# First two token tiles normalised one by one with ScalarE's square root, zero matmuls between their transposes, K and Q of the first eight heads alone, and a new issue order

## The chip, the cores and the metric

The kernel runs on one core of a Trainium2 chip. The metric is the device time of one execution in microseconds, less is better. Three runs of the kernel before gave 477.39, 476.0 and 477.12; their median is 477.12. The profile shows one execution, its times counted from its first instruction.

## The reference, cut to what matters

Two layers run over 2048 tokens of width 512. Each layer is an attention block (A) and a gated feed-forward block (B), with a layer normalisation ahead of either and a residual added behind it. The same weights serve both layers.

```python
def _layernorm(x):
    m = jnp.mean(x, axis=-1, keepdims=True); v = jnp.var(x, axis=-1, keepdims=True)
    return (x - m) / jnp.sqrt(v + 1e-05)

def _A_ref(x, wq, wk, wv, wo, beta):          # 32 heads of 16, N = 4 segments of L = 512 tokens
    q, k, v = ...                             # (B, H, N, L, 16)
    g = sigmoid(beta)
    for s in range(N):
        p = softmax(q_s k_s^T * scale + causal mask)
        o = g * (phi(q_s) M / (phi(q_s) z)) + (1 - g) * (p v_s)
        M, z = M + phi(k_s)^T v_s, z + sum phi(k_s)
    return concat(o) @ wo

def _B_ref(x, w1, w3, w2):                    # F = 1376
    return (silu(x @ w1) * (x @ w3)) @ w2

x = x + A(layernorm(x)); x = x + B(layernorm(x))      # layer 1
x = x + A(layernorm(x)); x = x + B(layernorm(x))      # layer 2
```

## The kernel before, in words

**The queues.** The kernel is written as a list of operations, each with the data that it reads and writes. Two texts then fix everything: `ORDER` gives the order in which all 3629 operations are issued, and `OTHER` names those that go to the second of their two allowed engines. (Emptying a PSUM bank, `ev`, may be done by ScalarE or by VectorE.) Each engine works through its own part of the list strictly in that order, and waits on semaphores ("lanes") for what the other engines owe it. There are 24 lanes: one for each of four engines, and eight for each queue that issues transfers (four in ScalarE's case). At the end SP waits once for every lane, sorted by lane number; a lane has its number from its first use. The last store to the output uses the lane numbered 11, so twelve lanes are waited for behind it.

**The stages.** Tokens go in segments of 512 (four tiles of 128), four segments in each of two layers. For each segment: layer normalisation; the transposed rows; Q, K and V (`project`); attention; output projection; normalisation; feed-forward. Work of neighbouring segments is interleaved by `ORDER`.

**Attention.** The heads are four groups G of eight. A unit is a batch of scores for 512 columns: TensorE (L897) writes them into PSUM, ScalarE takes the exponential (L906), GpSimd masks the diagonal blocks (L919), TensorE multiplies with V (L948). In the first segment a unit is cut in two halves of 1024 columns a row, and the segment's tokens are taken in two parts (tiles 0 and 1, then 2 and 3). There are 180 exponentials in all. The first unit reads K and Q of G = 0 and G = 1, with tiles 0 and 1.

**The head of the kernel**, which the change is about, runs so:

- Tiles 0 to 3 of x and the weights `wk` and `wq` are fetched. Later loads (tiles 4 to 7, `wv`, `w1`, `w3`, `wo`) are issued by SP once the third tile's statistics are done.
- Meanwhile TensorE multiplies zeros: seven operations `spin` of two 512-column matmuls (L524).
- `layer_norm(fine=True)` takes the tiles in pairs: VectorE's statistics (L635, L637) of both tiles, plus 1e-5 (L641), GpSimd's power -0.5 (L644), VectorE's two normalisations (L653), TensorE's four 128-column transposes for each tile (L665), and two copies out of PSUM, one on ScalarE (L493) and one on VectorE (L494).
- `project(first=True)` computes K and Q for tiles 0 and 1 with 256 columns a matmul (L226), two groups G to a bank: four jobs of eight matmuls. Banks are emptied by ScalarE (L493) or VectorE (L494); a masked copy of K for the odd heads (`km`, L738) is made by VectorE.
- ScalarE's own list begins: copy of tile 0's transposes, tanh for the gate (L615), K of G = 0, 1, Q of G = 0, 1, then exponentials.

Of the kernel before, what the change touches and what calls it, by code (L numbers as in the profile page):

```python
# [4 lines left out]
ALU = mybir.AluOpType  # L5
# [50 lines left out]
class Sched:  # L56
# [144 lines left out]
    def emit(self, nc, block):  # L201
# [49 lines left out]
def o_pe(ns):  # L251
# [7 lines left out]
    24 8 1 23 26 25 28 27 29 4 0 16 9 2 5 3 18 10 6-7 11 17 19 12 22 20-21 32 13-14 30 15 33 31 34 42 35 55 54 36  # L259
    56-58 39 37 43 40 38 41 44 84 45-47 51 65 94 66-68 75-76 69-70 77 71-72 78-82 85-91 61 73 83 74 163-164 161-162  # L260
    95 52 96-98 165 108-109 169-170 48 92 49 93 652 648 171 53 646 110 99-100 175 111 103 101 50 102 59-60 172 177
    650 176 166 123 178 124 167 112 168 173 180 179 104-105 181 113-114 182 653 649 651 647 654 115 183 125-126 106
    197 116-120 184 142 213 143 107 121 198 214 344 62 174 187 655 122 337 144 189 127-130 199 190 665 659 185
    200-201 131 145-146 132-137 211 660-661 138-140 235 151-153 212 236 186 345 233 203 348 147 202 204 662 346 350
    191 656 205 234 239-240 216 188 237 241-242 154 148 243 156 244 155 217 247 157 218-219 158 249 149 159 657 248
    250 150 160 251-252 717-720 663 666 238 658 253 215 347 245 255-256 664 667-671 349 721 352 141 257 63 192 353
    246 351 254 258 701 225 259 702 261 260 672 206 226 193-194 263 195 262 271-272 722 1080 264 207 1086 209 273-274
    208 1082 703-704 275 723 210 279 354-355 276 1084 1087 1081 1085 1083 280 673 277 724-725 285 674 278 675 281 356
    286 1088 220 705 1089 284 357 221 223 222 726 227 265 287 289 297 679 290 64 228 1093 229 1094 266 288 298 1091
    299 690 1090 196 691-692 300-302 693-694 684 303-304 1095 231 230 306 680-681 282 682 307-308 676 309 685-686 305  # L270
    310 224 683 677 687-688 311 695 678 696-698 706-707 1092 325 312 689 323 315 712 862 732 326 324 283 708-709 313
    291 699 314 267 232 733 736 734 710 316 292 1096 713-714 327-328 864 269 715-716 711 1097 749 329 1098-1099
    1106-1109 293-295 750 358-359 317 330 735 752-753 865 331 268 270 360 296 755 754 1100 361 1126 866 363 868 318
    737 362 364-367 1110 1127-1129 756 727-730 1111-1112 368 370 332 1130 371 369 861 757 319 1161 1113-1114 731 333
    863 342 372 738 760 1145-1148 1150 739 758 334 759 1115 1151-1152 867 761 1149 373 335 1153 1131 763 1132
    1121-1122 1140 1154 1160 740 321 336 320 322 375 764 751 1141-1142 1123 1143 1124 872 767 1133-1134 1144 1125 873
    374 1162 768 869-870 1135 741-742 376 1155-1156 1292 1157-1159 743-744 770 766 765 762 1101-1105 1136-1137 1139
    871 774-775 771 1290 1289 1293 377-378 784 379-380 382-385 381 785 1138 341 339 786 772-773 787 776 1291 777 700
# [123 lines left out]
def build(nc, A_x, A_wq, A_wk, A_wv, A_wo, A_beta, B_w1, B_w3, B_w2, out):  # L402
# [771 lines left out]
```

## Time and profile before

| what | value |
|---|---|
| median of three runs | 477.12 us (476.0 to 477.39) |
| span of the profiled execution | 476.0 us |
| time of that execution | 476.0 us, the span itself; one of the three runs shows the same figure |
| TensorE busy | 469.3 us, 99% |
| ScalarE busy | 390.6 us, 82% |
| VectorE busy | 385.3 us, 81% |
| GpSimd busy | 235.2 us, 49% |
| first exponential starts | 11.68 us |

Busy shares are means over stages with different limits. TensorE's ends are modelled (a matmul counts until its result has left the array), so that short gaps of it don't show as idle time. What bounds a stage is read from the chain of work in that stage and from who waits there.

### The profile page before, as it was taken

Reading aid. Unit: us, or ns where it says so; the run is one execution under the profiler, and the core shown is the slowest. Engines: PE = TensorE matmul, PEld = TensorE weight load, DVE = VectorE, ACT = ScalarE, POOL = GpSimd, SP = SyncE. Lnnn points to the kernel's source line nnn. Section 1 sums busy time; section 2 is a strip of 40 time slices with the busy share of each in tenths; the row PEclk is TensorE's granted clock in tenths of the full one; section 3 lists DMA queues with packets and bytes.
Section 4 is the critical chain, followed back from the end, with each engine's and each line's share of the span. In section 5 each row is a group of like instructions: output and inputs, shape, how many; then the busy total and the mean of one; then the engine's idle time right before and its main releaser. Section 6 shows DMA issues by size and latency. Waiting matters only on the chain.

```text
span 476.0 us, 14319 instructions
## 1 busy us (share of the span) xinstructions
PE 469.3 (99%) x6161; PEld 225.1 (47%) x6161; DVE 385.3 (81%) x818; ACT 390.6 (82%) x350; POOL 235.2 (49%) x382
## 2 busy tenths in 40 slices
PE   8999999999999999999999999999999999999997
PEld 4543456754443444444444344444444444444554
DVE  6899999897987977888987888787986677588582
ACT  2999999988999998999979999888989987930220
POOL 4756467746466556365464644644454655320000
DMA  8753349634134343251344416333132213332501
GB/s 263 265 101 74 66 91 195 113 67 56 23 68 90 68 90 62 48 84 36 67 83 85 68 24 107 63 68 64 31 64 44 45 34 67 69 39 48 119 14 56
DMA packets 106526, 37.14 MB, mean 78 GB/s; under 512 B 99200, under 2 KB 104448, under 8 KB 106464
## 3 DMA queue, kind: packets, MB, share of 16 engines
q1 hardware_dynamic: 104016, 31.41, 33.5%
q0 software_dynamic: 1488, 4.03, 3.9%
q8 instruction: 48, 0.79, 0.7%
q10 hardware_dynamic: 960, 0.79, 0.5%
q14 instruction: 14, 0.11, 0.1%
HBM read 8.43 MB, written 2.10 MB: 22 GB/s over the span
## 4 chain that ended last, share of the span: by engine, by line
PE 80%; ACT 11%; issue 3%; DVE 2%; DMA 2%; POOL 0%; POOLq 0%; DVEq 0%; SPq 0%
PE psall L226 48%; PE psall L231 15%; ACT e L906 9%; PE psall L897 9%; PE psall L948 6%; PE psall L524 1%; ACT px L755 1%; DMA W<-xn 1%; DMA xg<-xs 1%; PE psall L782 0%; DVE gp L1065 0%; DVE h L1069 0%; DVE W L759 0%; DVE xn L653 0%; ACT th L1063 0%
## 5 line engine op out<-in xcount | busy, mean ns | idle before, releaser
L906 ACT ACTIVATE e<-psall 128x2048 bf16<-128x2048 f32 (+1 forms) x180 | 300.5, 1697 | 26.1 <-PE psall L897 24.4
L919 POOL TENSOR_SCALAR_AFFINE_SELECT e<-e 128x512 bf16<-128x512 bf16 x256 | 157.5, 639 | 145.0 <-ACT e L906 97.5
L226 PE MATMUL psall<-W,w 128*128 128x512 bf16 (+1 forms) x499 | 106.9, 351 | 0.0
L226 PEld LDWEIGHTS psall<-W,w 128*128 128x128 bf16 x499 | 45.1, 98 | 44.4 <-issue 5.9
L1065 DVE SCALAR_TENSOR_TENSOR gp<-th,psall 128x512 bf16<-128x512 bf16 x80 | 54.0, 682 | 12.9 <-ACT th L1063 12.1
L1069 DVE SCALAR_TENSOR_TENSOR h<-gp,psall 128x512 bf16<-128x512 bf16 x80 | 54.0, 681 | 10.5 <-PE psall L226 6.3
L1063 ACT ACTIVATE th<-psall 128x512 bf16<-128x512 f32 x80 | 46.9, 600 | 16.1 <-PE psall L231 15.0
L226 PE MATMUL psall<-w,h 128*128 128x512 bf16 (+1 forms) x212 | 53.9, 380 | 0.0
L231 PE MATMUL psall<-W,w 128*32 128x512 bf16 (+1 forms) x884 | 48.8, 367 | 0.0
L635 DVE BATCH_NORM_STATS2 ln<-x_tok 128x6 f32<-128x512 bf16 x64 | 43.0, 686 | 1.7 <-DMA x_tok<-in_A_x_dram 1.0
L494 DVE CAST W<-psall 128x512 bf16<-128x512 f32 x51 | 34.6, 683 | 10.4 <-PE psall L226 9.9
L897 PE MATMUL psall<-W 16*128 16x256 bf16 (+3 forms) x544 | 41.3, 294 | 0.3
L948 PE MATMUL psall<-e,va 128*32 128x256 bf16 (+3 forms) x1088 | 41.2, 292 | 0.3 <-DVE rm L811 0.2
L897 PE MATMUL psall<-W,km 32*128 32x256 bf16 (+3 forms) x544 | 40.8, 291 | 0.0
L981 POOL TENSOR_TENSOR og<-xg,rd 128x256 bf16<-128x256 bf16 (+1 forms) x50 | 27.2, 559 | 24.4 <-DVE rd L975 16.6
L1088 DVE TENSOR_TENSOR x_tok<-psall,x_tok 128x512 bf16<-128x512 f32 (+1 forms) x33 | 21.7, 669 | 20.6 <-PE psall L231 11.1
L948 PEld LDWEIGHTS psall<-e,va 128*32 128x32 bf16 x1088 | 26.0, 96 | 17.5 <-issue 3.3
L231 PE MATMUL psall<-w,h 128*32 128x512 bf16 (+3 forms) x604 | 34.3, 364 | 0.0
L231 PEld LDWEIGHTS psall<-W,w 128*32 128x32 bf16 x884 | 23.4, 97 | 18.9 <-DVE h L1069 1.0
L494 DVE CAST xs<-psall 128x512 bf16<-128x512 f32 x40 | 26.7, 680 | 5.7 <-PE psall L948 5.6
L226 PE MATMUL psall<-wv,W 128*128 128x512 bf16 x110 | 31.3, 381 | 0.0
L897 PEld LDWEIGHTS psall<-W 16*128 16x128 bf16 x544 | 13.1, 91 | 37.8 <-ACT e L906 29.6
(85 smaller groups left out, 576.4 us busy)
## 6 DMA issues: line engine op xcount, KB each, us to landing
w<-in_B_w_dram SPq DMA_DIRECT2D x4, 688.0 KB, 8.3
out_dram<-x_tok SPq DMA_DIRECT2D x15, 128.0 KB, 2.1
km<-W POOLq DMA_DIRECT2D x24, 64.0 KB, 2.5
w<-in_B_w_dram POOLq DMA_DIRECT2D x3, 384.0 KB, 4.7
x_tok<-in_A_x_dram POOLq DMA_DIRECT2D x2, 512.0 KB, 4.7
xg<-xs SPq DMA_TRANSPOSE x36, 3.2
W<-og SPq DMA_TRANSPOSE x36, 2.5
wk<-in_A_wk_dram SPq DMA_DIRECT2D x1, 512.0 KB, 5.0
```

What stands on the lines that cost most here:

```text
L226: return e.matmul(out, lhsT, rhs, **k)
L231: o = e.matmul(out[c:c + 32], lhsT[:, c:c + 32], rhs, tile_position=(0, c), **k)
L494: return e.tensor_copy(dst(), src())
L635: dve(lambda e: e.bn_stats(ln_r[st.slot][:, i, 0:6], x_tok[:, tt, :]), 540, reads=[("x", tt)], writes=[(st, 0, i)], bufs=[st], prio=prio, ...
L897: o = e.matmul(S4[:, sps(pg), c:c + n], kk[32 * pg:32 * pg + r, G, 128 * j:128 * j + 128], q_r[z.q.slot][32 * pg:32 * pg + r, G, 128 * t1 ...
L906: act(lambda e, N=N, ebuf=ebuf, pgs=pgs, sps=sps: e.activation(e_r[ebuf.slot][:, pgs[0]:pgs[-1] + 1, 0:N], S4[:, sps(pgs[0]):sps(pgs[-1]) ...
L919: pool(lambda e, ebuf=ebuf, c=c: e.affine_select(e_r[ebuf.slot][:, :, c:c + 128], e_r[ebuf.slot][:, :, c:c + 128], pattern=[[0, 4], [1, 128]],
L948: o = e.matmul(bank(X)[32 * pg:32 * pg + 32, base + W - n:base + W], va_r[z.va.slot][:, j, h:h + 32], e_r[eb.slot][:, pg, c:c + n], start= ...
L981: return e.tensor_tensor(ogv()[:, 0:nt, :, k, :], src, v(1)[:, k, :, :, None].to_broadcast([P, nt, 4, DH]), ALU.mult)
L1063: act(lambda e, NW=NW, B=B, th=th: e.activation(th_r[th.slot][:, 0:NW], bank(B)[:, 0:NW], ACT.Tanh, scale=0.5), NW, reads=[(B, 0)], writes ...
L1065: dve(lambda e, NW=NW, B=B, th=th, gp=gp: e.scalar_tensor_tensor(gp_r[gp.slot][:, 0:NW], th_r[th.slot][:, 0:NW], 1.0, bank(B)[:, 0:NW], AL ...
L1069: dve(lambda e, NW=NW, B=B, gp=gps[fg], h=hs[fg]: e.scalar_tensor_tensor(h_r[h.slot][:, 0:NW], gp_r[gp.slot][:, 0:NW], 0.5, bank(B)[:, 0:N ...
```

## The change

1. `layer_norm(fine=True)` takes tile 0, then tile 1, each alone: statistics, a ScalarE square root of one column with 1e-5 as its bias (`lnsq`, the constants in a new tile `eps`), a VectorE reciprocal of one column (`lnrc`), the normalisation, the transposes. Tiles 2 and 3 stay a pair with GpSimd's power. The order by hand between statistics and normalisations (`hop`) goes.
2. The warm-up is eleven single 512-column matmuls in place of fourteen. Behind the transposes of tile 0 stands one zero matmul of 256 columns (`fill`), behind those of tile 1 three.
3. A one-column exponential (`tbl`) is put on ScalarE behind the two square roots.
4. The first half of `project` makes K and Q of G = 0 alone, then of G = 1 alone, then of G = 2, 3 together. The first three units of each pair of groups are arranged anew: the first unit needs G = 0 only.
5. At the end SP waits for the lanes in the order in which their last operations are issued; the last store is the last one.
6. `ORDER` and `OTHER` are new. The operations number 3644 (the numbers of those behind the first attention part are 15 higher). The last 2144 operations stand in the same order as before; the first 1485 of before are rearranged.

ScalarE's list up to the 52nd exponential, as the two texts give it (`e` is an exponential, L906, with its count; `phexp` is L755; `ev` copies a bank, K, Q, V, attention output X):

```
before  evt tanh-gate evK evQ e1-e10 phexp e11-e19 phexp e20-e37 phexp e38-e40 phexp e41 phexp e42 phexp e43 evV e44
        phexp e45 evK e46 phexp e47 phexp e48 evX tanhr e49 tanh evQ e50 tanh phexp tanh e51 tanh e52
after   lnsq lnsq evt tbl tanh-gate evK0 evQ0 e1-e12 phexp e13-e18 evV e19-e21 phexp e22-e37 phexp e38-e40 phexp e41 evQ
        phexp e42 phexp e43 evK e44 evV phexp e45 evK e46 phexp e47 evX evX e48 phexp e49 tanh tanhr e50 tanh phexp tanh
        e51 tanh e52
```

VectorE's list in the head goes: statistics of tile 0, those of tile 1, `cm`, reciprocal 0, `cm`, normalisation 0, reciprocal 1, normalisation 1, statistics of tile 2, copy of tile 1's transposes, the rest of tiles 2 and 3, `km` of G = 0. TensorE's: 11 spins, transposes 0, fill, transposes 1, three fills, 3 matmuls of K1, 4 of K0, 4 of Q0, 5 of K2, K1 and Q1, then the scores.

```diff
-        for op in self.ops:
-            finals[op.lane] = max(finals.get(op.lane, 0), op.val)
+        for op in self.issue:
+            finals.pop(op.lane, None)
+            finals[op.lane] = op.val
...
-                    for lane, v in sorted(finals.items()):
+                    for lane, v in finals.items():
...
 ORDER = """
-    24 8 1 23 26 25 28 27 29 4 0 16 9 2 5 3 18 10 6-7 11 17 19 12 22 20-21 32 13-14 30 15 33 31 34 42 35 55 54 36
...
+    178 102 177 103-104 95-97 93 105 98 69 63 106 109 61 179 110 180 111 22 189 27 107 183 70 112 667 190 184 64-65
...
+    eps = sb("eps", [P, 2], F32)
...
+    dve(lambda e: e.memset(eps[:], 1e-5), 1, writes=["eps"], prio=CP)
...
-    WARM = 7
...
-            for _ in range(2):
-                o = e.matmul(bank(B), xs_r[0][:, 0, 0:128], xs_r[0][:, 0, :], start=True, stop=True)
-            return o
...
+    WARM = 11
...
+    def spin(e, B=new("B")):
+        return e.matmul(bank(B), xs_r[0][:, 0, 0:128], xs_r[0][:, 0, :], start=True, stop=True)
...
+    def fill(n, op):
+        for _ in range(n):
+            op = pe(lambda e: e.matmul(bank(wb)[:, 0:256], xs_r[0][:, 0, 0:128], xs_r[0][:, 0, 0:256], start=True, stop=True),
+                    256 / 1.2, reads=["warm"], writes=[(wb, 0)], bufs=[wb], after=[op], name="fill")
+            pools["xs"].prev[0].append(op)
+        return op
...
-        for a, b in ([(0, 2), (2, 4)] if fine else [part]):
-            for i in range(a, b):
+        def root_act(i):
+            act(lambda e: e.activation(ln_r[st.slot][:, i, 8:9], ln_r[st.slot][:, i, 7:8], ACT.Sqrt, bias=eps[:, 0:1]), 1, False,
+                reads=[(st, 1, i), "eps"], writes=[(st, 2, i)], bufs=[st], prio=prio, name="lnsq")
+            dve(lambda e: e.reciprocal(ln_r[st.slot][:, i, 9:10], ln_r[st.slot][:, i, 8:9]), 8, reads=[(st, 2, i)],
+                writes=[(st, 3, i)], bufs=[st], prio=prio, name="lnrc")
+
+        if fine:
+            for i in range(2):
                 stats(i)
-            root(a, b)
-            turned(a, b)
+                root_act(i)
+                turned(i, i + 1)
+                filled[0] = fill((1, 3)[i], flips[i])
+            act(lambda e: e.activation(eps[:, 1:2], eps[:, 0:1], ACT.Exp), 1, False, reads=["eps"], writes=["eps1"], prio=prio,
+                after=[S.res_w[(st, 2, 1)]], name="tbl")
+            part = (2, LT)
+        for i in range(*part):
+            stats(i)
+        root(*part)
+        turned(*part)
...
-                for A in (0, 2):
-                    jobs += [("k", (A, A + 1), hf), ("q", (A, A + 1), hf)]
+                for Gs in ((0,), (1,), (2, 3)) if hf == 0 else ((0, 1), (2, 3)):
+                    jobs += [("k", Gs, hf), ("q", Gs, hf)]
...
-                if t1 == 2 and G < EVEN_FIRST:
-                    out += [([(G, 0, 1), (G + 1, 0, 1), (G, 0, 0)], []), ([(G + 1, 0, 0), (G, 1, 1), (G + 1, 1, 1)], []),
-                            ([(G, 1, 0), (G + 1, 1, 0)], [(G, (0, 1)), (G + 1, (0, 1))])]
+                if t1 == 2:
+                    out += [([(G, 0, 0), (G, 0, 1), (G, 1, 1)], []), ([(G, 1, 0), (G + 1, 0, 0)], [(G, (0, 1))]),
+                            ([(G + 1, 0, 1), (G + 1, 1, 0), (G + 1, 1, 1)], [(G + 1, (0, 1))])]
```

## Rows read from the trace of the kernel before

**Rows 1.** The page, part 1: busy time of each engine.
```profile
PE 469.3 (99%) x6161; PEld 225.1 (47%) x6161; DVE 385.3 (81%) x818; ACT 390.6 (82%) x350; POOL 235.2 (49%) x382
```

**Rows 2.** The chain that ended last, 0 to 60 us: start, length, what.
```profile
1.26 6.10 PE psall L524 x14
7.36 0.46 PE psall L665 x8
...
8.32 2.90 PE psall L226 x25
...
11.24 0.42 PE psall L897 x15
...
11.68 9.27 ACT e L906 x10
```

**Rows 3.** Stages: busy PE, PEld, DVE, ACT, POOL; granted clock; DMA share; GB/s.
```profile
11.68:31.00 19.32, 19.09 (x251) 9.63 (x255) 16.78 (x38) 19.32 (x22) 13.79 (x22) 1.00 0.62 206
31.00:51.50 20.50, 20.34 (x329) 8.59 (x329) 19.51 (x51) 20.47 (x24) 11.39 (x22) 1.00 0.46 82
...
75.00:85.00 10.00, 9.80 (x185) 7.09 (x186) 9.83 (x24) 9.93 (x12) 6.24 (x11) 1.00 1.05 211
...
105.00:120.00 15.00, 15.00 (x162) 6.49 (x158) 11.59 (x23) 13.07 (x10) 8.04 (x14) 1.00 0.45 65
```

**Rows 4.** ScalarE's waits, 11 to 85 us: total, times, longest.
```profile
ACT e L906 <- PE psall L897: 0.6, 1, 0.6
```

**Rows 5.** TensorE's weight loads, their waits, 11.2 to 51.5 us.
```profile
PEld psall L897 <- ACT e L906: 8.8, 26, 0.4
```

**Rows 6.** The chain's shares by line, 100 to 213 us.
```profile
by line: PE psall L226 65.3%; PE psall L897 12.9%; PE psall L231 12.7%; PE psall L948 8.9%; PE psall L782 0.4%
```

**Rows 7.** VectorE in order of time: start, length, line, operation, count, wait ahead.
```profile
3.62 1.29 DVE L635 BATCH_NORM_STATS2 ln<-x_tok 128x6 f32<-128x512 bf16 x2 [0.97 <-DMA x_tok<-in_A_x_dram]
...
5.16 0.17 DVE L641 TENSOR_SCALAR ln<-ln 128x2 f32<-128x2 f32 x1
5.37 0.69 DVE L635 BATCH_NORM_STATS2 ln<-x_tok 128x6 f32<-128x512 bf16 x1
6.16 0.73 DVE L653 TENSOR_SCALAR xn<-x_tok,ln 128x512 bf16<-128x512 bf16 x2
...
7.84 0.42 DVE L494 COPY W<-psall 128x512 bf16<-128x512 bf16 x1 [0.86 <-PE psall L665]
```

**Rows 8.** GpSimd in order of time, 0 to 14 us.
```profile
5.42 0.70 POOL L644 TENSOR_TENSOR ln<-ln,mhalf 128x2 f32<-128x2 f32 x1 [0.36 <-DVE ln L641]
```

**Rows 9.** ScalarE in order of time, 0 to 24 us.
```profile
2.75 1.28 ACT L493 ACT_TABLE_LOAD   x1 [2.75 <-issue]
7.62 0.60 ACT L493 ACTIVATE W<-psall 128x512 bf16<-128x512 bf16 x1 [3.59 <-PE psall L665]
8.22 0.23 ACT L615 ACTIVATE gth<-betab 128x32 f32<-128x32 bf16 x1
9.95 1.14 ACT L493 ACTIVATE W<-psall 128x512 bf16<-128x512 f32 x2 [1.51 <-PE psall L226]
```

**Rows 10.** Transfers: KB each, us from issue to landing.
```profile
wq<-in_A_wq_dram ACTq DMA_DIRECT2D x1, 512.0 KB, 6.3
...
wv<-in_A_wv_dram SPq DMA_DIRECT2D x1, 512.0 KB, 4.8
```

**Rows 11.** ScalarE's groups by line and shape: busy, mean ns, idle ahead.
```profile
L1036 ACT ACTIVATE th<-psall 128x192 bf16<-128x192 f32 x16 | 5.1, 332 | 17.7 <-PE psall L231 16.5 <-PE psall L226 1.1
L493 ACT ACTIVATE W<-psall 128x512 bf16<-128x512 f32 x13 | 7.6, 598 | 1.7 <-PE psall L226 1.7
```

**Rows 12.** SP's issues in order of time, 472 to 476 us.
```profile
472.50 1.27 SPq L484 DMA_DIRECT2D out_dram<-x_tok  x2
```

**Rows 13.** SP's waits from 462 us on.
```profile
SPq L217 <- DMA out_dram<-x_tok: 1.1, 1, 1.1
```

More of the change, by code (lines that the diff above doesn't have):

```diff
@@ L516, in clear_slot @@
         pools["va"].prev[i] = [z, pool(ones, 128, **k)]
-    WARM = 7
-    if WARM:
-        dve(lambda e: e.memset(xs_r[0][:, 0, :], 0.0), 200, writes=["warm"], prio=CP - 1)
-        def spin(e, B=new("B")):
-            for _ in range(2):
-                o = e.matmul(bank(B), xs_r[0][:, 0, 0:128], xs_r[0][:, 0, :], start=True, stop=True)
-            return o
-        wb = spin.__defaults__[0]
-        pools["xs"].prev[0] = [pe(spin, 2 * MM512 * (2 if i < 4 else 1), reads=["warm"], writes=[(wb, 0)], bufs=[wb], prio=1e4, name="warm")
-                               for i in range(WARM)]
+    WARM = 11
+    dve(lambda e: e.memset(xs_r[0][:, 0, :], 0.0), 200, writes=["warm"], prio=CP - 1)
+    def spin(e, B=new("B")):
+        return e.matmul(bank(B), xs_r[0][:, 0, 0:128], xs_r[0][:, 0, :], start=True, stop=True)
+    wb = spin.__defaults__[0]
+    filled = [None]
+    def fill(n, op):
[4 more added lines that the diff above has]
+        return op
+    pools["xs"].prev[0] = [pe(spin, 2 * MM512, reads=["warm"], writes=[(wb, 0)], bufs=[wb], prio=1e4, name="warm")
+                           for i in range(WARM)]
     SPINS = 0
@@ L651, in turned @@
                 if k == 0:
-                    xn = new("xn")
+                    pair[0] = new("xn")
+                xn = pair[0]
                 op = S.add([o_dve(512, False, 1.45)], lambda e, i=i, k=k, tt=tt, xn=xn: e.tensor_scalar(
@@ L666, in flip @@
                         return o
-                    pe(flip, 4 * 62, reads=[(xn, k), "ident"], writes=[(B, 0)], bufs=[B, xn], prio=-900, name="xt")
+                    flips[i] = pe(flip, 4 * 62, reads=[(xn, k), "ident"], writes=[(B, 0)], bufs=[B, xn], prio=-900, name="xt",
+                                  after=filled if fine and i == 1 else [])
                     ev(lambda i=i: dt_[dst.slot][:, i, :].rearrange("p (g c) -> p g c", c=P), tb, 512, reads=[(B, 0)], writes=[(dst, i)],
@@ L724, in project @@
                     pe(fn, W / 2.4 + 2.5, mode="F", reads=rd + ["w" + kind], writes=[(B, 0)], bufs=[B, X],
-                       prio=p0 + 0.001 * cg + 0.004 * a - 500, gates=[gate],
+                       prio=p0 + 0.001 * cg + 0.004 * a - 500, gates=[gate], after=filled if first else [],
                        hold=[{"q": z.q, "k": z.k, "v": z.va}[kind]] + ([z.km] if kind == "k" and g <= 1 else []), name="%s%d.%d" % (kind, G, cg))
@@ L734, in project @@
             part = lambda t, Gs=Gs, c0=c0, c1=c1: t[:, Gs[0]:Gs[-1] + 1, c0:c1]
-            ev(lambda b=b, part=part: part(w_r[b.slot]), lambda B=B, m=len(Gs): bank(B).rearrange("p (g c) -> p g c", g=m), 512,
+            ev(lambda b=b, part=part: part(w_r[b.slot]), lambda B=B, m=len(Gs), W=W: bank(B)[:, 0:W * m].rearrange("p (g c) -> p g c", g=m), W * len(Gs),
                reads=[(B, 0)], writes=[(b,) + x for x in keys], bufs=[B, b], prio=p0 - 100, name="ev" + kind)
@@ L865, in build @@
     JOIN = True
-    EVEN_FIRST = 0
     HP = -1e6
```

274 lines of the change are left out of this document (139 added, 135 removed), and 16 rows, old and new, of the table OTHER.

## The prediction

> **What bounds the kernel now.** I read the page's busy shares first: TensorE shows 99% [rows 1], but its ends are modelled, so this says little about a stage. I then followed the chain of work, and the stages. Three stretches appear. Up to 11.68 us nothing but the head is on the chain: 14 zero matmuls, 8 transposes, 25 K and Q matmuls, 15 score matmuls, then the first exponential [rows 2]. From 11.68 to about 85 us ScalarE is busy all the time [rows 3] and waits 0.6 us in total [rows 4]: it sets the pace, while TensorE's score loads wait 8.8 us for exponentials in 26 places [rows 5]. VectorE is nearly as full there (19.51 of 20.50 us, 9.83 of 10). Later the chain holds TensorE alone [rows 6], and ScalarE has idle time again (13.07 of 15 us busy between 105 and 120 [rows 3]). So a microsecond saved in the head is a microsecond by which ScalarE's unbroken run starts earlier; it reaches the end only if that run isn't made longer before TensorE takes over.
>
> **The change: the head.** VectorE's first statistics wait for tile 0 until 3.62 us; two take 1.29, 0.6 apart [rows 7]. That start stays.
> - Removed from the chain: the statistics of tile 1 before the root of tile 0, the addition (0.17, [rows 7]), GpSimd's power (0.70, [rows 8]).
> - Added: ScalarE's root (nearest row: a 32-column ACTIVATE, 0.23 [rows 9]; between none and twice that, the transposes move by 0.2 at most) and a one-column reciprocal, taken as 0.1.
> - Tile 0: statistics to 4.3, aggregate to 4.5, root to 4.8. VectorE meanwhile does tile 1's statistics (to 5.15) and a `cm`, then the reciprocal, an aggregate, a `cm`; normalisation 0 (0.73 for two in sequence, so about 0.4 each, [rows 7]) ends at 6.0, normalisation 1 at 6.5. Before, they ended at 6.6 and 6.9.
> - TensorE: 14 spins took 6.10 us [rows 2], 0.436 each for 512 columns, which is the 1.2 GHz level. Eleven end at 6.05. So the transposes of tile 0 start at 6.1, where before they started behind the spins at 7.2, though normalised data lay ready. The spins, not the normalisation, were last; shortening both is what makes the gain.
> - Four transposes: eight filled the 0.46 us between the spins' end and the copy [rows 2], so 0.25 for four, or 0.45 at the low level. Taking the low one, tile 0's are done at 6.5 and ScalarE copies them (0.60, [rows 9]) to 7.15. The fill and tile 1's transposes run to 7.2; VectorE, held by tile 2's statistics (0.69) until 7.2, copies them (0.42) by 7.75 [rows 7]. The three zero matmuls (0.64 low, 0.33 high) end by 7.85. They cost nothing beyond that 0.1, since K waits for the copy anyway; without that cover they would cost 0.33 to 0.64.
> - K starts at 7.85 (before: 8.32). 25 K and Q matmuls took 2.90 us [rows 2], 0.116 each for 256 columns, which is the 2.4 GHz level; the granted clock column shows 1.00 in each stage [rows 3] and doesn't tell the two levels apart, the pace of the rows does. Before, all 25 stood ahead of the scores; now Q of G = 0 is the eleventh: 1.3 us, so 9.15, and 0.2 to leave the array. `wq` lands at 1.71 + 6.3 = 8.0 [rows 10], Q's first matmul comes at 8.65: covered.
> - ScalarE: the exponential needs another table than the root. One load is 1.28 us [rows 9]. It stands behind the copy: 7.15 to 8.45. Then `tbl` and the gate's tanh, 0.23 each, to 8.9. K0's bank has 256 columns: between 332 ns for 192 and 598 for 512 [rows 11], so 0.38: to 9.3. Q0 to 9.6. The load hides behind the transposes of tile 1, its copy and the K matmuls; what is queued behind it is K0's copy, whose data is ready at 8.85, so only 0.05 us shows.
> - From the end of ScalarE's Q copy (9.95 + 1.14 = 11.09, [rows 9]) to the first exponential 0.59 passed. The same again gives 10.2 against 11.68: **1.5 us earlier**.
> - Moved: SP's later loads hang on tile 2's statistics, which now end at 7.2 instead of 6.06. `wv`, second in that queue, is issued at 7.65 and lands 4.8 later [rows 10], at 12.45; V's first matmul stands behind the fifth half unit, whose bank comes free with the third exponential, at 13.1 (ten take 9.27, [rows 2]): 0.6 to spare. Tiles 4 to 7 ahead of it in SP's queue and `w1`, `w3`, `wo` behind it come 1.1 us later too. Were V later than 13.1, the score matmuls queued behind it on TensorE, and ScalarE after them, would wait by the difference. I take 0.
>
> A rule that speaks against this is weighed here. The row shows a load of 1.28 us and a first use 3.59 us after it, put down to TensorE's transposes [rows 9], so the trace doesn't show what a switch costs an engine that has work waiting. The Trainium skill, page ScalarE: Activation LUTs, section What ACT_TABLE_LOAD costs, says that every switch to another set costs the load, about 1283 ns, and about 1380 ns of drain, 2.66 us together. The load agrees with the row. By the rule the first exponential would come 1.4 us later, at about 11.6, and the estimate of the time would be 476.9.
>
> **The new order.** Counted on ScalarE's list, three more banks are emptied by ScalarE ahead of the 52nd exponential than before: a V behind the 18th, a K behind the 43rd, an attention output behind the 47th. Two copies in 1.14 us [rows 9] make 0.54 each: 1.6 us more in the stretch where ScalarE never waits. VectorE, nearly as full, loses the same three copies. The bounds are 0 (what waits for VectorE comes earlier by as much) and 1.6 (ScalarE alone sets the pace to the last). I take 0.5, nearer to 0, because TensorE's own score loads show 8.8 us of waits [rows 5] from which an order can regain, and because beyond 85 us the lag falls into ScalarE's idle time (1.9 us between 105 and 120, [rows 3]). In the last 2144 operations the order is the same.
>
> **The end.** SP's last issue ends at 473.77 [rows 12]; it waits 1.1 us for the store [rows 13], to 474.9. The span ends at 476.0. In those 1.1 us lie the twelve lanes that stand behind the last store's and the closing of the program. With the new order of waits no lane stands behind it. Bounds 0 and 1.1; I take 0.6, the middle: the rows don't part the waits from the closing.
>
> **The sum.** -1.5 + 0.5 - 0.6 = -1.6. The profiled execution took 476.0, so 474.4 by its own measure; the median of the runs is 1.1 above it, and the forecast for the median is 477.1 - 1.6 = **475.5**. A measurement of this kernel tells 0.3%, 1.43 us, from no change: 475.7 to 478.5 counts as the same.
>
> **The rivals.**
> - *Paid back.* ScalarE's 1.6 us of extra copies eat the whole head gain; only the end remains: 477.1 - 0.6 = 476.5. For it: ScalarE's 0.6 us of waits to 85 us. Against: VectorE's relief.
> - *The new order regains more.* TensorE's waits for exponentials are 8.8 us in 40 us; a quarter less gives 2.2 more: 473.3.
> - *The table switch is dear*, which ends on the other side. Place: between tile 0's copy and K0's copy on ScalarE. The rows bound it by 1.28 (the load) and 4.87 (from the load's start to the next ACTIVATE, 2.75 to 7.62). Each microsecond beyond the load delays the first exponential by one. At 4.87 it comes at 13.8: 479.1. It is slower by over 0.3% from 3.0 us beyond the load. For it: no row shows a switch under pressure. Against: the row blames the wait on the transposes. With 1.4 beyond, as in the page's figure cited above, it is 476.9, the same.
> - *The clock stays low.* TensorE ran 6.1 us of unbroken zero matmuls at the 1.2 GHz level before it ran K at 2.4. Now the unbroken stretch is 4.8 us, then transposes with gaps. If K0, K1 and Q0 run low, 11 matmuls cost 0.116 more: 1.3 us, 476.8. If it stays low to about 16 us, TensorE falls 3 us of work behind and it is slower, 478.6.
> - *The new order is worse*: scores reach ScalarE late in the first 200 us. With a third more of the 8.8 us it is +1.3 in sum, 478.4; more makes it slower.
>
> **How the numbers follow.** The forecast 0.38, its own range 474.6 to 476.2 (0.31 of it beyond 0.3%); regains more 0.22; paid back 0.15; dear switch 0.11 (0.04 slower); low clock 0.08 (0.03 slower); worse order 0.06 (slower). So faster 0.53, same 0.34, slower 0.13. The range goes from 472.6, which leaves out the far end of the third kind, to 478.3, which leaves out the slower ends.
>
> **What would show it.** Two table loads, the second right behind tile 0's copy and K0's copy right behind the tanh (if a gap stands there, the switch is dear). First spins ending near 6.0, K from 7.9 at 0.11 a matmul (0.21: low clock). First exponential near 10.2 and ScalarE unbroken to 31 us. At 85 us the same work should be done about 1 us earlier; if it is level with before, the payback was whole. Behind the last store's landing 0.5 us instead of 1.1. The prediction is wrong if the first exponential isn't before 11, or if TensorE's waits between 50 and 200 us grow.

## The result and the profile after

The changed kernel takes 479.93 us (median of four runs, 479.54 to 480.24), the kernel before 477.00 in the same comparison (four runs, 476.0 to 477.39). The ratio on record is 1.0071, with a 95% interval of 1.0056 to 1.0087: slower by 0.7%. Between the medians it is 2.9 us, 0.6%. The forecast was 475.5, the range 472.6 to 478.3. Both the sign and the range were wrong. The profiled execution of the changed kernel has a span of 478.2 us and took 479.91.

Page, part 1, of the changed kernel (it answers to [rows 1]):

```profile
PE 465.5 (97%) x6166; PEld 224.0 (47%) x6204; DVE 384.9 (80%) x819; ACT 393.8 (82%) x355; POOL 239.7 (50%) x384
```

ScalarE has 3.2 us more work, TensorE is busy 3.8 us less in a span that is 2.2 us longer. It waits somewhere. (`W<-xn` below is the transposing transfer of normalised rows that SP issues and TensorE's next products wait for.)

The head first. ScalarE in order of time, changed kernel (start, length, line, what, wait ahead), which answers to [rows 9]:

```profile
6.63 0.60 ACT L501 ACTIVATE W<-psall 128x512 bf16<-128x512 bf16 x1 [0.99 <-PE psall L679]
7.24 1.28 ACT L702 ACT_TABLE_LOAD   x1
8.54 0.20 ACT L702 ACTIVATE eps<-eps 128x1 f32<-128x1 f32 x1
8.65 0.21 ACT L630 ACTIVATE gth<-betab 128x32 f32<-128x32 bf16 x1
8.77 0.78 ACT L501 ACTIVATE W<-psall 128x256 bf16<-128x256 f32 x2
10.04 1.94 ACT L934 ACTIVATE e<-psall 128x1024 bf16<-128x1024 f32 x2 [0.49 <-PE psall L925]
```

and the chain of the changed kernel from 0 to 60 us, answering to [rows 2]:

```profile
1.29 4.87 PE psall L531 x11
...
7.76 1.91 PE psall L227 x16
```

The first exponential starts at 10.04 us, 1.64 earlier than before [rows 2]. Over all traces of this case the old head has it at 11.30 to 11.68 us (six traces) and the new one at 9.46 to 10.07 (nine), so the gain is no accident of these two traces, but either head scatters by about half a microsecond. The second table load stands directly behind the copy, and what follows it starts 0.02 us after its end.

To find where this lead goes I numbered the exponentials in both traces and subtracted the starts, changed kernel minus before. Between two of them, ScalarE's list tells what was added. The table is worked out from ScalarE's instructions in order of time.

| from, to | before, us | after, us | lag at its end | what differs on ScalarE |
|---|---|---|---|---|
| start, e1 | 11.68 | 10.04 | -1.64 | the head |
| e1, e31 | 29.58 | 30.83 | -0.39 | one bank (V) more, 0.62; waits 0.54 against 0.03 |
| e31, e49 | 31.95 | 33.22 | +0.88 | three banks more, 1.82; one tanh fewer, 0.35 |
| e49, e53 | 11.24 | 10.96 | +0.60 | one bank fewer, one tanh more |
| e53, e57 | 10.31 | 11.31 | +1.60 | waits 1.13 against 0.28 |
| e57, e73 | 40.07 | 40.56 | +2.09 | waits 4.64 against 3.89 |
| e73, e85 | 31.25 | 32.75 | +3.58 | waits 2.73 against 1.30 |

From e85 (166 us) to e180 (414 us) the lag stays between 3.57 and 3.58. So the change is decided in the first 166 us: a lead of 1.64 becomes a lag of 3.58. Up to e53 three banks more on ScalarE (1.84 in all) and half a microsecond of new waits take up the lead and 0.6 besides. Behind that TensorE waits. The waits of TensorE from 31 to 200 us (total, times, longest), of the changed kernel and then of the kernel before:

```profile
PE psall L227 <- DMA W<-xn: 2.3, 2, 1.2
```

```profile
PE psall L948 <- DVE rm L811: 0.2, 1, 0.2
```

Stages (columns as in [rows 3]), of the changed kernel and then of the kernel before, where these two stretches were not shown:

```profile
31.00:51.50 20.50, 20.23 (x328) 8.46 (x318) 16.63 (x44) 20.50 (x23) 14.41 (x26) 1.00 0.43 85
...
85.00:120.00 35.00, 33.54 (x467) 19.52 (x469) 29.42 (x60) 30.77 (x25) 23.93 (x36) 1.00 0.43 79
...
120.00:165.00 45.00, 43.12 (x507) 19.00 (x509) 36.22 (x78) 41.21 (x37) 26.71 (x42) 1.00 0.31 58
```

```profile
85.00:120.00 35.00, 34.91 (x486) 19.91 (x478) 29.70 (x62) 31.38 (x26) 21.75 (x34) 1.00 0.46 74
120.00:165.00 45.00, 45.00 (x496) 19.82 (x489) 38.73 (x84) 43.66 (x39) 24.82 (x39) 1.00 0.34 66
```

TensorE, which was full before, is busy 1.4 and 1.9 us less in these two stretches. From 31 to 51.5 ScalarE is full as before. VectorE has room there: it is busy 16.63 us where it had been 19.51 [rows 3], and waits for 3.6. Its waits in this stretch, changed kernel:

```profile
DVE W L502 <- PE psall L227: 1.9, 1, 1.9
DVE xn L669 <- POOL ln L659: 1.1, 1, 1.1
```

The first of TensorE's two waits is for rows normalised at 82 us. VectorE there, in order of time, of the kernel before and then of the changed one:

```profile
77.23 0.48 DVE L641 TENSOR_SCALAR ln<-ln 128x2 f32<-128x2 f32 x1
...
81.56 0.41 DVE L653 TENSOR_SCALAR xn<-x_tok,ln 128x512 bf16<-128x512 bf16 x1
...
82.08 0.40 DVE L653 TENSOR_SCALAR xn<-x_tok,ln 128x512 bf16<-128x512 bf16 x1
```

```profile
80.64 0.16 DVE L656 TENSOR_SCALAR ln<-ln 128x2 f32<-128x2 f32 x1
...
82.62 0.41 DVE L669 TENSOR_SCALAR xn<-x_tok,ln 128x512 bf16<-128x512 bf16 x1 [0.17 <-POOL ln L659]
82.94 0.68 DVE L1093 SCALAR_TENSOR_TENSOR gp<-th,psall 128x512 bf16<-128x512 bf16 x1
83.54 0.41 DVE L669 TENSOR_SCALAR xn<-x_tok,ln 128x512 bf16<-128x512 bf16 x1
```

The new order adds 1e-5 3.4 us later, and puts another instruction between the two normalisations; the transposing transfer is issued 1.5 us later, of which 0.6 is the lag at e53.

A late issue is only a part of either wait. The chain of the changed kernel shows the two transfers for which TensorE waits (start, length, what):

```profile
83.98 4.47 DMA W<-xn
...
133.47 4.80 DMA W<-xn
```

In the kernel before they are issued at 82.51 and 131.01 and take 3.65 and 3.16 us. Take off the lag, 0.60 at e53 and 2.09 at e73: the first is issued 0.9 late and takes 0.8 longer, the second is issued 0.4 late and takes 1.6 longer. Queue and transfer of the changed kernel while the second is on its way, 133.4 to 138.3 us:

```profile
q8 instruction: 1, 0.02, 1.2%
...
W<-xn SPq DMA_TRANSPOSE x1, 4.8
```

Between 130.9 and 134.2 us, where the kernel before has the same transfer on its way, there is no packet of the queue named "instruction". The one packet of this queue, 16 KB, runs from 136.26 to 137.19 in the trace of the changed kernel. Of the sixteen parts of the transfer fifteen have landed by 136.70, the last lands at 138.28. During the first transfer such a packet runs from 86.62 to 87.58. TensorE had run out of other work at 87.39 and at 137.30. Estimates from these rows: of the two waits, 2.3 us together, about 0.4 would be left with the durations of before, and about 1.1 with the longer durations but an issue that is late by the lag alone. That the packet makes the transfer long is not shown by an edit; the last section has the count over all traces.

The end. SP's waits from 462 us on, changed kernel (answering to [rows 13]), and its last issues (answering to [rows 12]):

```profile
SPq L218 <- DMA out_dram<-x_tok: 0.5, 2, 0.4
```

```profile
474.70 1.79 SPq L492 DMA_DIRECT2D out_dram<-x_tok  x2
```

The wait falls from 1.1 to 0.5, as forecast. But the two issues take 1.79 us instead of 1.27, and all of the difference is in the last (0.85 instead of 0.33), so that from the end of VectorE's last instruction to the end of the trace it is 2.56 us where it was 2.64.

One thing about the trace of before must be known for reading the lags. It holds a late wait of TensorE, from 436 to 456 us:

```profile
PE psall L231 <- DMA W<-xn: 1.1, 1, 1.1
```

The profiled execution of the changed kernel has no such wait, and of seven other traces with the old order throughout (below) six have none. It is the main reason why a lag of 3.57 at 414 us is only 2.2 in the span. Traces of one and the same order differ on the way too: that of the end alone (below), whose order is that of before, lags by 0.78 at e45 and by another 1.1 at e55. So a step of this size between two single traces proves nothing by itself. The times of the kernel before lie in two groups about 1.2 us apart: of 23 runs on one chip, 13 from 475.92 to 476.54 and 10 from 477.20 to 477.79. Wherever a run's time and span are both known, the time is 1.7 to 1.9 us above the span; so the profiled execution before, whose span is 476.0, belongs to the upper group, and its time is near 477.8, not 476.0.

### The profile page after: what moved, and what is told of

It reads as the page before. It is cut to its first block, busy times and chain, and to the rows that moved or that the text cites. A ratio compares the mean times of both kernels' runs of the same rounds, so it can differ in the third digit from the quotient of the medians.

```text
span 478.2 us, 14380 instructions
## 1 busy us (share of the span) xinstructions
PE 465.5 (97%) x6166; PEld 224.0 (47%) x6204; DVE 384.9 (80%) x819; ACT 393.8 (82%) x355; POOL 239.7 (50%) x384
## 4 chain that ended last, share of the span: by engine, by line
PE 83%; DVE 10%; ACT 3%; DMA 2%; issue 1%; POOL 1%; DVEq 0%
PE psall L227 45%; PE psall L232 20%; PE psall L925 10%; PE psall L976 6%; ACT e L934 2%; DMA W<-xn 2%; DVE ln L650 2%; DVE W L502 1%; PE psall L531 1%; DVE x_tok L1029 1%; DVE W L788 1%; DVE xn L669 1%; DVE xs L502 1%; ACT px L784 1%; DVE W L786 1%
## 5 line engine op out<-in xcount | busy, mean ns | idle before, releaser
L947 POOL TENSOR_SCALAR_AFFINE_SELECT e<-e 128x512 bf16<-128x512 bf16 x256 | 159.3, 646 | 128.7 <-ACT e L934 80.1
L227 PE MATMUL psall<-W,w 128*128 128x512 bf16 (+1 forms) x498 | 108.5, 351 | 1.7 <-DMA W<-xn 1.2
L227 PE MATMUL psall<-w,h 128*128 128x512 bf16 (+1 forms) x198 | 50.8, 380 | 1.5 <-issue 0.8
L1009 POOL TENSOR_TENSOR og<-xg,rd 128x256 bf16<-128x256 bf16 (+1 forms) x51 | 28.5, 571 | 34.8 <-DVE rd L1003 18.6
L502 DVE CAST W<-psall 128x512 bf16<-128x512 f32 (+1 forms) x53 | 35.3, 674 | 10.2 <-PE psall L227 10.0
L232 PE MATMUL psall<-w,h 128*32 128x512 bf16 (+2 forms) x596 | 33.6, 364 | 0.0
L227 PE MATMUL psall<-W,wq 128*128 128x512 bf16 (+1 forms) x127 | 32.2, 358 | 0.1
L659 POOL TENSOR_TENSOR ln<-ln,mhalf 128x4 f32<-128x4 f32 (+1 forms) x17 | 16.7, 981 | 29.0 <-DVE ln L656 23.2
```

Source lines behind the costliest of these rows:

```text
L227: return e.matmul(out, lhsT, rhs, **k)
L232: o = e.matmul(out[c:c + 32], lhsT[:, c:c + 32], rhs, tile_position=(0, c), **k)
L502: return e.tensor_copy(dst(), src())
L947: pool(lambda e, ebuf=ebuf, c=c: e.affine_select(e_r[ebuf.slot][:, :, c:c + 128], e_r[ebuf.slot][:, :, c:c + 128], pattern=[[0, 4], [1, 128]],
L1009: return e.tensor_tensor(ogv()[:, 0:nt, :, k, :], src, v(1)[:, k, :, :, None].to_broadcast([P, nt, 4, DH]), ALU.mult)
```

## The experiments

**The end alone.** The kernel before with the new order of waits at the end.

```diff
-        for op in self.ops:
-            finals[op.lane] = max(finals.get(op.lane, 0), op.val)
+        for op in self.issue:
+            finals.pop(op.lane, None)
+            finals[op.lane] = op.val
...
-                    for lane, v in sorted(finals.items()):
+                    for lane, v in finals.items():
```

> The kernel before with one edit: SP's waits at the end stand in the order in which the lanes' last operations are issued. The prediction: 0.6 us less than before, 476.4. Rival, from the changed kernel's trace, where 2.6 us lie between VectorE's last instruction and the end of the span as they did before: no change, 477.0.

476.92 us (10 runs) against 476.88, ratio 0.9993 (0.9975 to 1.0011): no difference that can be measured. SP's waits and last issues of this kernel:

```profile
SPq L218 <- DMA out_dram<-x_tok: 0.5, 1, 0.5
```

```profile
473.56 1.27 SPq L485 DMA_DIRECT2D out_dram<-x_tok  x2
```

Here the issues take no longer than before, and from VectorE's last end to the end of the trace it is 2.05 us instead of 2.64. All five traces with the old waits show 2.62 to 2.64; of twelve with the new waits nine show 2.03 to 2.07, and three, that of the changed kernel among them, 2.46 to 2.62, each with a last issue of 0.74 to 0.90 us. So the gain of 0.6 is there in most executions, and in some a slower issue of the store takes it back; by the ratio of the times it is 0.3, which ten runs do not separate from nothing.

**The normalisation alone.** The changed kernel's normalisation, warm-up and end, with the K and Q jobs, units and order of before.

```diff
-                for Gs in ((0,), (1,), (2, 3)) if hf == 0 else ((0, 1), (2, 3)):
-                    jobs += [("k", Gs, hf), ("q", Gs, hf)]
+                for A in (0, 2):
+                    jobs += [("k", (A, A + 1), hf), ("q", (A, A + 1), hf)]
...
-                if t1 == 2:
+                if t1 == 2 and G < 0:
```

> The normalisation of the changed kernel alone (tiles 0 and 1 one by one, ScalarE's root, spins, zero matmuls, end waits), with the K and Q jobs, the units and the issue order of the kernel before. Transposes' copy at 7.66 instead of 8.26, so the first exponential at 11.1, a lead of 0.6 us. Theory 1 (a lead of the head reaches the end, and what the change lost was lost by the order behind it): 476.3. Theory 3 (a lead of the head is worth nothing, since ScalarE and VectorE together set the pace up to 85 us and the lead is waited away): 476.9. Theory 2 (the head harms): above 478.

476.92 us (10 runs) against 476.46 (19 runs), ratio 0.9997 (0.9983 to 1.001). Its first exponential is 0.59 earlier than in the trace of before, which is the latest of the six with the old head, and 0.40 of that is left at e180. So a small lead arrives in this trace, but it is too small to be measured beside the two groups of times.

**How far the new order goes.** Four kernels have the changed head; they follow the new order up to an exponential, and then the old order and engines.

```diff
 ORDER = """
...
-(after's list behind the exponential e6, e22, e41 or e53)
+(before's list from there on, with what is left of it)
```

> The changed kernel with the new issue order only up to the sixth exponential; behind it every operation stands in the order, and on the engine, of the kernel before. Theory 1 (the head gains what was forecast, and the order behind it loses it again): the first exponential is at 10.0 us, the lead of 1.6 us lasts to TensorE's stretch, and the time is 475.0 to 475.9. Theory 2 (the head itself does the harm, by later loads or by a switch of tables): 479 or more, as with the whole change.

> The same with the new order up to the 22nd exponential (31 us). Theory 1 with the loss spread over the whole order: about a third of the way from the first kernel of this call to the whole change, 476.5. Theory 1 with the loss behind 50 us alone (three more banks emptied by ScalarE, a later normalisation): as the first kernel of this call but for the one V copy on ScalarE, 475.5 to 476.1. Theory 2: 479 or more.

> The same with the new order up to the 53rd exponential (85 us). The changed kernel was 0.6 us behind before at this exponential, having been 1.6 ahead at the first, and fell another 3 us back between it and the 83rd. Theory 1: the lag at the 53rd exponential is 0.6 us again and the time is 477.5, or 478.5 if TensorE then waits for the late normalisation as in the changed kernel. Theory 2: 479 or more.

> The changed kernel with the new order up to the 41st exponential (52 us), the order and engines of before behind it. The version cut at the 53rd had a lead of 0.3 us at the 41st exponential and a lag of 0.5 to 0.8 between the 45th and the 53rd, then 1.8 from the 57th to the end. Theory 1, with the loss behind the 41st due to the new order: the lead of 0.3 lasts, 476.6. Theory 3: the old order too loses time after 52 us when it comes in with other leads of the engines: 478 or more.

The two early cuts tell nothing of the order and leave both theories open, because the joint itself stalls. Up to e6: 483.6 us, ratio 1.0138 (1.0115 to 1.0161). The new units do not fit the old order of the masks; TensorE waits, and then its clock falls. Waits from 20 to 29.5 us, and stages, of that kernel:

```profile
PE psall L967 <- POOL e L938: 3.0, 1, 3.0
```

```profile
20.00:29.30 9.30, 5.65 (x90) 2.90 (x91) 6.31 (x14) 6.19 (x7) 6.94 (x12) 1.00 0.41 105
29.30:36.00 6.70, 6.37 (x37) 2.74 (x36) 3.06 (x6) 4.01 (x4) 1.75 (x3) 0.50 0.19 39
```

The granted clock is 0.50, the 1.2 GHz level, for the 6.7 us after the stall. Up to e22: 486.59 us, in the trace at 0.50 from 36.9 to 57.4 us; one run of four without the fall took 478.86.

In the later cuts the clock stays at 1.00. Up to e41: 478.22 us against 476.46, ratio 1.0035 (1.0024 to 1.0046); the lag goes from -2.12 at e1 to -0.55 at e41 and +0.27 at e45, and stays at +0.24 to +0.39. Up to e53: 478.84 against 476.88, ratio 1.0044 (1.0028 to 1.0059); -1.61 at e1, +0.51 at e53, and one step of 1.3 at e55 with the late rows of 82 us; +1.81 at the end. So the kernel with the first 41 exponentials' order already loses the lead and more; in the traces the other cut ends 1.4 later (1.81 against 0.39), 1.3 of it in the step at e55, and the changed kernel 1.8 later than that (3.57 against 1.81). The step at e55 comes with the old order too: it is 1.1 us in the end alone and in the kernel before with the small copy (below), where the transfer of 82 us takes 5.4. The ratios, 1.0035, 1.0044 and 1.0071, stand in the same order, but those of the two cuts are not separate, and the trace of the first is its fastest run (477.6).

Behind e41 the first of them has K's and X's banks on VectorE again, and it loses as much from e41 to e53 (0.82) as the changed kernel (0.87), 0.65 of it as new waits of ScalarE for scores before e45. That is the third theory on record, 478 or more: the old order too loses time here when it is entered with other leads of the engines. The joint may have a part in it. So 1.84 us says where ScalarE's time went, not what another place for the copies would give back.

**The banks back.** The changed kernel with the three banks (V behind e18, K behind e43, X behind e47) emptied by VectorE, as before.

```diff
 OTHER = """
...
+    170 790 1130
```

> The changed kernel with three banks (a V behind the 18th exponential, a K behind the 43rd, an attention output behind the 47th) emptied by VectorE again, at the same places of the order. If these three copies on ScalarE were the loss, the first lead of 1.6 us is kept to the 53rd exponential but for the 0.7 lost before the 17th, and the time is 478.3 or less. If VectorE, which is on the chain from 50 to 83 us in the changed kernel, is the bound there, three more copies of 0.68 on it make it later: 480 to 481.5.

482.27 us, ratio 1.0112 (1.0092 to 1.0132): 2.3 slower than the changed kernel by the medians, 2.0 by the ratios, and beyond both expectations. ScalarE's waits from 10 to 140 us, of this kernel and then of the changed one:

```profile
ACT e L929 <- PE psall L920: 8.1, 15, 1.1
```

```profile
ACT e L934 <- PE psall L925: 4.5, 9, 0.9
```

My theory that ScalarE's copies are a loss that can be taken back falls. In this order VectorE comes too late to them, the scores wait for the banks, and ScalarE waits 3.6 us more for the scores. Of the two places for these copies ScalarE is the cheaper one.

**Is VectorE too full?** Eight statistics between 12 and 40 us over 64 columns, in the changed kernel and in the kernel before. The statistics of these rows are left incomplete.

```diff
+            c = 64 if name == "xa" and prio in (0.0, 1.0) else 512
-            dve(lambda e: e.bn_stats(ln_r[st.slot][:, i, 0:6], x_tok[:, tt, :]), 540, reads=[("x", tt)],
+            dve(lambda e: e.bn_stats(ln_r[st.slot][:, i, 0:6], x_tok[:, tt, 0:c]), 540, reads=[("x", tt)],
```

> The changed kernel, with the attention normalisation's statistics of segments 1 and 2 in layer 1 taken over 64 of the 512 columns (eight VectorE instructions, each about 0.68 us, down to about 0.15; the statistics of these rows are left incomplete). It takes about 4 us of VectorE's work out of 12 to 40 us. Theory that VectorE's lateness in this stretch eats the head's gain: the 45th exponential starts 1 to 2 us earlier than in the changed kernel, the end too, 478 to 479. Rival, that only the two waits of TensorE for late rows at 84 and 138 us make the loss: under 0.5 us gained, 479.4 to 479.9.

> The same eight statistics over 64 columns in the kernel before (left incomplete). If VectorE is late only in the new order: under 0.5 us gained, 476.4 to 476.9. If VectorE sets the pace in the old order as much as in the new: 1 to 2 us gained, 475 to 476, like the changed kernel with the same edit.

Groups of VectorE's instructions, 10 to 45 us, of the first of the two:

```profile
L651 DVE BATCH_NORM_STATS2 ln<-x_tok 128x6 f32<-128x64 bf16 x8 | 1.6, 211 | 0.0
```

That is 3.8 us less work (8 times 0.69 less 0.21). The changed kernel with it takes 479.48 us, ratio to before 1.005 (1.0034 to 1.0065), where the changed kernel had 1.0071. In the trace it starts 0.58 earlier, which is scatter of the head (the first shortened statistics come at 11.9 us, e1 at 9.46), gains another 0.36 by e45, and has 0.43 of both at the end. The kernel before with it takes 477.34 against 477.32, ratio 1.0009 (0.9993 to 1.0025), and its lag to the trace of before is constant, -0.38 at e1 and -0.39 at e53. So in the old order 3.8 us of VectorE's work are worth nothing, and in the new order hardly anything: its load is not the bound, though in the kernel before it is busy 19.51 of 20.50 us [rows 3]. That the moment at which single instructions come counts instead is likely, but no run shows it.

**Does a shift in the head arrive?** ScalarE copies with unused output between e1 and e2: two of 1024 columns in the kernel before, one of 512 in either kernel.

```diff
+    wait = [op for op in S.ops if op.name == "ldwq"]
+    wait = [act(lambda e: e.activation(px_r[0][:, 0:1, :], wq_sb[:, 0:1, :], ACT.Copy), 512, False, writes=["late"], after=wait, name="late")]
+    pools["px"].prev[0] = wait
```

> The kernel before with two copies of 1024 columns on ScalarE between the first and the second exponential; they write a scratch tile and take 1.9 us. If a microsecond of the head is a microsecond of the end, as the prediction had it: 478.8. If the slack of TensorE and of the order up to 85 us takes it up: under 477.5.

> The kernel before, with one more ScalarE copy of 512 columns (about 0.6 us, output unused) between the first and the second exponential. Theory that the head's time reaches the end one for one: 0.6 us more than before, about 477.4, and a lag of 0.6 at every later exponential. Theory that VectorE with ScalarE sets the pace up to 85 us, so that small shifts of the first exponentials are swallowed on the way: lag 0.6 at the 5th exponential, under 0.2 at the 45th and at the end, 476.8 to 477.0.

> The same copy in the changed kernel, between its first and second exponential. One for one: 0.6 us more than the changed kernel, about 480.5. Swallowed on the way, since VectorE is what is late in the new order: a lag of 0.6 at the 5th exponential against the changed kernel, under 0.2 at the 45th, and 479.9 to 480.1 at the end.

Yes, and one for one. The small copy delays e2 by 0.52 more than e1 in both. In the kernel before that difference is still 0.51 at e53. In the changed kernel, against its own trace, ScalarE's first waits take it up, but it is back at 0.58 by e17, and is 0.67 at e45 and 0.57 at e180. My second theory, that the new order swallows shifts of the head, falls with it. The times show less: 477.73 against 477.32 (ratio 1.0006, 0.9993 to 1.0019), and 480.1 (1.0065, 1.0046 to 1.0083). The large copies cost far more than their 2.1 us: 482.65 us, and 479.36 in the one run of four in which the clock did not fall. Stages of the profiled execution:

```profile
12.00:16.90 4.90, 2.67 (x23) 1.02 (x23) 2.55 (x6) 4.87 (x6) 1.42 (x3) 1.00 1.03 408
16.90:27.20 10.30, 9.94 (x90) 4.38 (x89) 5.10 (x15) 7.31 (x8) 5.98 (x9) 0.50 0.34 96
27.20:40.00 12.80, 12.40 (x206) 6.42 (x204) 10.84 (x27) 12.21 (x14) 8.35 (x13) 1.00 0.46 100
```

**The late rows earlier.** Both late normalisations of the changed order earlier; the first of them earlier in the kernel before; and that on top of the normalisation alone. Only places in the order differ.

```diff
 ORDER = """
...
-(405 ... 788 ... 426 ... 802 407 ... 408 ... 409 410)
+(405 406 ... 407 788 ... 426 408 409 ... 1310 410 ... 802)
...
-(1230 919 ... 1219 ... 1605 ... 921 920 922 ... 923 924 925)
+(919 1230 ... 1219 921 920 922 923 924 925 ... 1605)
```

> The changed kernel; only the place of two normalisations in the issue order is different (those whose transposed rows TensorE waits for at 87 and at 138 us): the addition of 1e-5, GpSimd's power, the normalisations and the transposing transfers stand a few instructions earlier, so that the first transfer is issued about 3 us earlier (84.0 to about 80.5) and the second pair about 1 us earlier. Theory that these late rows make the part of the loss behind the 53rd exponential: TensorE's two waits for W<-xn (1.2 us each) are gone, and the end comes 1.5 to 2.4 us earlier than in the changed kernel, 477.5 to 478.4, still 0.5 to 1.5 slower than before. Rival, that everything is late there and another wait takes their place: under 0.5 us gained, 479.4 to 479.9.

> The kernel before, with the first of these two normalisations about 2 us earlier in the same way. In its traces this one transfer takes 3.4 to 3.6 us in some executions and 5.4 in others, and then TensorE waits 1.0 to 1.1 us. If that is what spreads its times over 476.0 to 478.6: times within 476.0 to 477, median 476.3 to 476.6 (ratio about 0.999). If the spread has another cause: the same median and spread as before, 477.0 to 477.3.

> The kernel with the new normalisation of the first two tiles, the new warm-up and the new end waits, but the old K and Q jobs and the old order (first exponential about 0.5 us earlier than before, measured equal to before), and on top of it the first of the two normalisations about 2 us earlier. If a head gain reaches the end one for one in the old order and the late transfer adds about 1 us in half the executions: median 475.8 to 476.2, ratio 0.997 to 0.9985. If not: 476.9, the ratio 0.9997 that it had without this edit.

All three missed. The changed kernel with earlier rows takes 482.72 us, ratio 1.014 (1.0122 to 1.0158), 2.8 more than without (3.3 by the ratios). Its waits, first of TensorE from 31 to 165 us, then of ScalarE from 10 to 140 us:

```profile
PE psall L232 <- DVE W L496: 1.2, 1, 1.2
PE psall L227 <- DVE x_tok L1110: 1.1, 1, 1.1
PE psall L805 <- DMA W<-W: 0.9, 1, 0.9
```

```profile
ACT e L928 <- PE psall L919: 7.6, 12, 1.8
```

The waits for `W<-xn` are gone, as expected (the two transfers take 3.2 and 3.4 us here), and others of the same size have come. The first instructions moved ahead cost 1.1 us at e53, before the rows matter at all, 0.6 more by e57 and another 2.4 by e73. In the kernel before the same move brings the transfer forward only from 82.51 to 81.71 (half of that is this trace's earlier start), because SP is still busy with other transposes; e53 is 0.64 later than e49 would have it; 477.91 us against 476.37, ratio 1.0018 (1.0006 to 1.003). On top of the normalisation alone: 476.48, ratio 1.0005 (0.9993 to 1.0016). The two groups of times stay.

## Why the prediction was wrong

**The head was right.** Spins to 6.16 (6.05 was forecast), copy to 7.23 (7.15), table load to 8.52 (8.45), K from 7.76 (7.85) at 0.119 us a matmul, which is the 2.4 GHz level, K0's copy at 8.77 (8.9), first exponential at 10.04 (10.2). The term of -1.5 measured -1.64; of the "clock stays low" rival nothing came. The switch costs its load alone: the row shows 1.28 us and the next instruction 0.02 later. The Trainium skill, page ScalarE: Activation LUTs, section What ACT_TABLE_LOAD costs, gives about 1380 ns of drain besides. An estimate by this figure puts the first exponential near 11.4; it started at 10.04, so the trace does not agree here.

**"A microsecond saved in the head reaches the end if the run isn't made longer" was right too**, in the order of before: shifts of 0.38 and 0.52 us pass through 53 exponentials unchanged.

**The step that failed is the cost of the new order.** I bounded it by 0 and 1.6 and took 0.5, "nearer to 0", from two arguments. The first was that TensorE's score loads wait 8.8 us for exponentials [rows 5], from which an order could regain. In the changed kernel these waits are 6.6 us from 10 to 51.5, yet nothing is regained, for a load that waits for an exponential while ScalarE never waits [rows 4] is only ScalarE's pace seen from the other side. The second was that the lag falls into ScalarE's idle time beyond 85 us; the lag does not shrink there. Up to e53 the term is 2.24 us instead of 0.5: 1.84 for the three banks, which alone is over the upper bound of 1.6, and 0.46 for ScalarE's new waits make 2.30 of it. The bound took 0.54 for a bank from two copies in a row; a copy between exponentials costs 0.6. The loss is no accident of one trace: from e1 to e53 the four traces that keep the new order so far (its own, the cut at e53, the eight statistics, the small copy without its own 0.52) lose 1.9 to 2.4 us, those with the old order 0.0 to 0.8.

**Behind e53 the "worse order" rival came true**, at 0.06 the least likely of all. I named its mechanism as scores that reach ScalarE late. The place is another: TensorE waits 1.2 and 1.1 us for transposed rows, and 3.0 us are lost between e53 and e85. Rows whose normalisation stands later in the order are the smaller part of these waits; the transfers of the rows took 0.8 and 1.6 us longer than before. The list of ScalarE that I compared ended at the 52nd exponential, and I took the rest of the first 1485 operations as free. The second sign of being wrong that I had named came: TensorE's waits between 50 and 200 us grew from 0.2 to 3.5 us.

**The end** was put at -0.6. In most traces with the new waits it is -0.6; in that of the changed kernel the last store's slower issue leaves -0.1.

In the sum: -1.64 in the head, +2.24 to e53, +2.98 to e85, together +3.58 at e85, and -0.1 at the end. The traces' spans differ by 2.2, mostly because that of before holds the wait of 1.1 at 445 us; the medians, over both groups of times, differ by 2.9.

**What stays open.** Which of the rearrangements behind the 53rd exponential could be spared was not found. Each single move, banks back or rows earlier, made the kernel slower, so the waits named here show where the time is lost, but not that removing them would give it back. No run changes the two transfers' durations alone, so how much of the 3.0 us is theirs stays an estimate. No version was found that is measurably faster than the kernel before.

## What to carry to other kernels

Where an engine never waits for a long stretch, count the instructions that a new order gives it and charge each in full, as the upper bound, up to the place where another engine takes over; waits that others have for this engine are no reserve. Compare the whole rearranged part of the order, not the list of one engine up to some count, and look for producers that stand later ahead of a stretch that another engine bounds. Where rows come late, split the delay into a later issue and a longer transfer before blaming the order. A wait seen in a trace is not a term of a sum until the experiment that removes it has made the kernel faster.

## What the hardware showed that was not expected

TensorE's granted clock fell from 1.00 to 0.50 after single stalls in the first 30 us: after a wait of 3.0 us, for 6.7 us, and with ScalarE's two added copies, after a wait of 2.2 us, for 10.3 us. In this second kernel the lag grew from 1.81 at e5 to 6.2 at e13, so that the fall cost twice what the stall did.

One transposing transfer has several durations in otherwise equal programs. It is the one issued at 82 to 83 us. Transfers from 81 to 90 us (count, us from issue to landing), of the kernel before, of the kernel before with the small copy, and of the changed kernel:

```profile
W<-xn SPq DMA_TRANSPOSE x1, 3.6
```

```profile
W<-xn SPq DMA_TRANSPOSE x1, 5.4
```

```profile
W<-xn SPq DMA_TRANSPOSE x1, 4.5
```

With 5.4 TensorE waits 1.0 us, and the profile puts it down to VectorE's `gp`, of which one ends at 88.32, just before the matmul starts at 88.33:

```profile
PE psall L226 <- DVE gp L1061: 1.0, 1, 1.0
```

But in the kernel before the same matmul starts at 86.94, and that `gp` ends only at 88.00: the matmul does not need it. The transfer's landing at 88.20 fits, 0.13 us ahead of the start, as in the changed kernel (88.44 and 88.58). Together with the transfer at 440 us, whose wait of 1.1 us comes in some executions only, this fits the two groups of times: of the seven traces with the old order throughout and no clock fall, the four with spans of 476.0 to 476.5 hold one of these two waits, the three of 474.0 to 475.0 neither.

What goes with the long durations is a packet of the queue named "instruction". The 17 traces hold 474 transfers `W<-xn` with their landing. In 294 of them no packet of that queue overlaps the transfer, and they took 3.0 to 3.5 us. The other 180 took 3.0 to 5.6, and all 55 that took over 4.3 are among them. The second transfer for which the changed kernel waits took 4.75 to 4.83 us in all four traces with the new order throughout (its own, the banks back, the eight statistics, the small copy), and 3.1 to 3.2 wherever the old order stands there. Why the packet meets it in the new order each time is open.
